# The last softmax chain of a fused attention and mixture kernel: reading from PSUM, turning over a diagonal, and small matmuls in the pauses

## The chip, the cores and the metric

The kernel runs on one core of one Trainium2 chip. The metric is device time in microseconds of one execution. A core has TensorE (matmul, with its own loading of weights), VectorE, ScalarE, GpSimd and SyncE; SyncE issues the DMA transfers here. PE, DVE, ACT, POOL and SP are the profile's names for them.

## The reference, cut to what matters

```python
def attn(q, k, v):                      # 4 batches, 8 heads, 576 tokens, 64 wide
    s = q @ k.T / 8
    s = where(s >= kth_largest(s, 32), s, -1e9)
    return softmax(s) @ v

def moe(x, phi, w1, w2):                # x 2304 x 512, 8 experts of 4 slots
    logits = x @ phi                    # 2304 x 32
    d = softmax(logits, axis=0)         # over all tokens, for each slot
    slot_input = d.T @ x                # 32 x 512
    slot_out[e] = relu(slot_input[e] @ w1[e]) @ w2[e]
    return softmax(logits, axis=1) @ slot_out

def moe2(x, w_in, w_out):
    h = x @ w_in
    g = where(h >= 1, h, where(h <= -1, 0, (h + 1) ** 2 / 4))
    return g @ w_out                    # 2304 x 512

out = moe2(moe(attn(q, k, v)))
```

## The kernel before

The attention runs over 16 pairs of heads (two heads at a time, four pairs for a batch), each in five rows of blocks of queries. Tokens of work (a letter for the step, two digits for row and half, the pair after the dot) are laid out in a repeating order for the frames, and for the last frames in a list written by hand, `TAIL`. In these stretches the order on TensorE, VectorE, ScalarE and GpSimd is exactly that of the list. The kernel's weights (w1, w2, w_out and helpers, 512 KB a tile, some loaded as two halves of 256 KB) come by a stream of loads from SyncE (`wload`, L196), in one fixed order, into buffers that come free during the attention. At most eight are in flight. Each load waits until what its buffer held is no longer read, and since SyncE issues in order, the loads behind wait with it.

The softmax over tokens is done batch by batch with a running maximum (`nmn`, negated), a running sum (`run_q`, then `run_s`) and a running weighted sum `acc` (partitions are pair and slot, columns the two heads' values): at each batch, acc = acc x al + new, where al is the exponential of the change of the maximum. For the last batch this chain stands at the end of `TAIL`, after the last attention matmuls (L550); it is called the drain here. It works in three pieces of tokens, n = 0 and 1 of 256 tokens each and n = 2 of the last 64 (the mid piece). The steps, with the lines of the kernel before, are:

- `na`, `nb`: logits of the piece on TensorE, one matmul for each of the four pairs of the batch, the last one in `nb` (L757). They go into one PSUM tile `lm_ps` of three banks, one bank for a piece.
- `nc`: ScalarE copies the logits to `lT` in SBUF (L760). `nl`: a copy of a part to `lall` for the later combine (L770).
- `nd`: VectorE takes the maximum (L764) and joins it to the running one (L765).
- `ne`: ScalarE's exponential into `eT`, with the sum (L773). `nf`: the factor `al` (L777).
- `nt`: TensorE turns `eT` (L782, and L285/L287 for the mid piece). `ng`: ScalarE copies the turned piece to `et` (L794) or `er` (L791).
- `nw`: the weighing, TensorE multiplies the turned exponentials with the tokens' values `xh` (L721), into the same bank. `nx`: VectorE, acc = acc x al + that (L798). `ny`: the running sum (L800).
- `jp`, `jd`: `run_q` of the earlier batches to `run_s`. `sp`: TensorE transposes `acc` to `si_ps` (L737). `sa`: ScalarE copies that to `siT` (L739).

With `siT` the experts begin: `h` from w1 (L1049), `so` from w2 (L1072), then the combine. The preparation of w_out (on ScalarE, GpSimd and VectorE) and moe2 follow, the last matmuls into `o_ps` (L1255).

Of the kernel before, what the change touches and what calls it, by code (L numbers as in the profile page):

```python
# [77 lines left out]
Y01.14 m09.11 C30.14 z4.14 O11.14 K10.14 T30.13 Q30.13 S31.14 U31.13 B0.14 L2.14 X10.14 K11.14  # L78
E31.13 m10.11 X11.14 C31.14 P00.14 G30.14 Y10.14 U40.13 T31.13 G31.14 M20.14 P01.14 Q31.13 M21.14
Y11.14 A20.13 L3.14 S40.14 R3.13 A21.13 O20.14 U00.14 K20.14 E40.13 C40.14 B1.14 O21.14 T40.13  # L80
Q40.13 X20.14 c0.15 c1.15 S00.15 E00.14 M30.14 K21.14 P10.14 T41.13 G40.14 H2.13 R4.13 U01.14 X21.14
V30.14 c4.15 Y20.14 K30.14 Q41.13 A30.13 P11.14 C00.15 T00.14 E01.14 S01.15 U10.14 Q00.14 M31.14
A31.13 C01.15 E10.14 U11.14 H3.13 Y21.14 T01.14 B2.14 Q01.14 R0.14 V31.14 Y30.14 S10.15 L4.14 X00.15
C10.15 T10.14 S11.15 P20.14 K31.14 Y31.14 E11.14 c5.15 U20.14 Q10.14 C11.15 A40.13 G01.15 P21.14
A41.13 H4.13 M40.14 L0.15 c2.15 B3.14 T11.14 V40.14 lD.13 S20.15 A00.14 U21.14 R1.14 A10.14 P30.14
K40.14 G10.15 E20.14 C20.15 M00.15 Q11.14 Y40.14 P31.14 lN.13 A01.14 T20.14 E21.14 Q20.14 S21.15
H0.14 M01.15 B4.14 A11.14 T21.14 U30.14 C21.15 O01.15 H1.14 S30.15 K01.15 R2.14 Q21.14 G11.15 K00.15
L1.15 E30.14 G20.15 lX.13 X01.15 T30.14 M10.15 U31.14 C30.15 A20.14 c6.15 E31.14 Y00.15 Y01.15
M11.15 B0.15 P40.14 Q30.14 S31.15 lC.13 C31.15 O11.15 U40.14 G21.15 X10.15 K10.15 L2.15 K11.15
T31.14 P01.15 R3.14 P00.15 M20.15 U01.15 A21.14 E40.14 Q31.14 U00.15 M21.15 V20.15 X11.15 S40.15  # L90
H2.14 T40.14 A30.14 E01.15 E00.15 Y10.15 Q40.14 Y11.15 G30.15 B1.15 C40.15 V21.15 A31.14 P10.15
H3.14 T41.14 T00.15 T01.15 U10.15 P11.15 R4.14 Q41.14 A40.14 K20.15 Q00.15 K21.15 A41.14 R0.15
G31.15 Q01.15 E10.15 L3.15 nm3.15 Y20.15 H4.14 P30.15 U11.15 A00.15 Y21.15 B2.15 lD.14 E11.15 A01.15
P20.15 M30.15 T10.15 T11.15 rd0.15 H0.15 R1.15 lY.13 Q10.15 G40.15 lE.13 P31.15 lN.14 M31.15 lX.14
V30.15 Q11.15 K30.15 lC.14 Y30.15 U20.15 E20.15 U30.15 fl0.15 A10.15 V31.15 A11.15 L4.15 rd1.15
lY.14 T30.15 K31.15 P21.15 lE.14 Y31.15 T20.15 H1.15 U31.15 M40.15 na0.15 Q30.15 Q20.15 fl1.15
U21.15 E21.15 T31.15 T21.15 R3.15 A30.15 Q31.15 nm4.15 V40.15 R2.15 K40.15 P40.15 Q21.15 Y40.15
U40.15 A31.15 B4.15 A20.15 A21.15 rd3.15 rd2.15 T40.15 B3.15 H3.15 xc1.15 xc0.15 H2.15 T41.15 Q40.15
Q41.15 R4.15 nb0.15 nc0.15 nd0.15 nl0.15 fl3.15 fl2.15 A40.15 xc2.15 A41.15 rd4.15 na1.15 ne0.15
# [10 lines left out]
def kernel_body(tc, qT, kT, vP, phi, w1, w2, w_in, w_out, out, fast, flag):  # L110
# [633 lines left out]
    def last_mix(k, n):  # L744
# [8 lines left out]
        turned = bank[:, :(NR + 1) * NSLOT].rearrange("p (r s) -> p r s", s=NSLOT)  # L753
# [7 lines left out]
        elif k == "d":  # L761
            mb = p_moe.tile([P, 1], F32, name="mb", tag="mb", bufs=3)
            nm = p_moe.tile([P, 1], F32, name="nmn", tag="nmn", bufs=4)
            nc.vector.reduce_max(mb, lT[:, c0:c1], axis=AX.X)  # L764
# [6 lines left out]
        elif k == "e":  # L771
            sb = p_moe.tile([P, 1], F32, name="sb", tag="sb", bufs=3)
            nc.scalar.activation(eT[:, c0:c1], lT[:, c0:c1], AF.Exp, bias=sums[n]["nm"], scale=1.0, accum_out=sb)  # L773
# [5 lines left out]
        elif k == "t":  # L779
            eye = ident[:NSLOT, :NSLOT]  # L780
            for r in main:
                nc.tensor.transpose(turned[:, r, :], eT[:NSLOT, r * P:(r + 1) * P], eye)  # L782
            if mid:
                for jj in range(2):
                    sl = slice(jj * REM, (jj + 1) * REM)
                    flip(turned[sl, NR, :], eT[:NSLOT, NR * P:], eye, jj)
        elif k == "g":
            if mid:
                for jj in range(2):
                    sl = slice(jj * REM, (jj + 1) * REM)  # L790
# [658 lines left out]
```

## Time and profile before

| | us |
|---|---|
| median of three runs | 773.25 (772.62 to 773.60) |
| the profiled execution | 771.83 |
| its span in the profile | 770.0 |
| TensorE busy | 736.8 (96%) |
| VectorE busy | 651.0 (85%) |
| ScalarE busy | 612.2 (80%) |
| GpSimd busy | 491.7 (64%) |
| chain that ended last: TensorE, VectorE, GpSimd, DMA | 58%, 24%, 7%, 6% |

A number of a view is from the profiled execution, in us from the start of its span. The busy share of an engine is a mean over stages that have different limits, so a change at one place is read in the rows of that place: which engine works, what the others wait for, and who waits for them. The stages that matter here: attention with the hand-written list to about 479 us, the drain to about 490, the experts to about 530, and moe2 to the end.

### The profile page before, as it was taken

The page shows a single profiled execution, that of the slowest core. Times are in us where ns is not written, and L with a number is a line of the kernel's source. Part 1 is how long each engine was busy: PE and PEld are TensorE (multiplying, and loading weights), DVE is VectorE, ACT ScalarE, POOL GpSimd, SP SyncE. Part 2 cuts the span into 40 slices and gives each one's busy share as a digit, 9 for nine tenths or more (in the row PEclk, how much of TensorE's full clock was granted, in tenths as well). Part 3 has the DMA queues.
Part 4 walks back from the last instruction along what each step waited for, and adds up shares of the span by engine and source line. Part 5 has one row for each costly group of instructions (what it writes and reads, how often), then busy time and mean ns, then how long its engine had stood idle before and what let it go on. Part 6 is the DMA issues. An engine that isn't in the chain of part 4 may idle for free.

```text
span 770.0 us, 15917 instructions
## 1 busy us (share of the span) xinstructions
PE 736.8 (96%) x5014; PEld 542.5 (70%) x5014; DVE 651.0 (85%) x2924; ACT 612.2 (80%) x1300; POOL 491.7 (64%) x532
## 2 busy tenths in 40 slices
PE   4899999999999999999999999898999999999996
PEld 2477777677777677777777788334577788888885
DVE  5999999999999999999999996173899967776662
ACT  4799999999999999999999997243788864554542
POOL 2899999999999999999999995030455400000000
PEclk9899999999999999999999999899999999999998
DMA  7414314304304302202202137999600020100101
GB/s 230 144 59 149 105 47 150 132 25 150 129 22 151 136 19 96 83 15 96 82 20 96 46 105 273 334 406 406 269 0 1 0 83 1 43 10 33 41 1 45
DMA packets 32013, 81.50 MB, mean 106 GB/s; under 512 B 5680, under 2 KB 6576, under 8 KB 31920
## 3 DMA queue, kind: packets, MB, share of 16 engines
q1 hardware_dynamic: 31632, 79.94, 29.1%
q8 instruction: 41, 0.67, 0.4%
...
q14 instruction: 52, 0.43, 0.2%
...
## 4 chain that ended last, share of the span: by engine, by line
PE 58%; DVE 24%; POOL 7%; DMA 6%; issue 2%; ACT 1%; SPq 1%; DVEq 0%; POOLq 0%; ACTq 0%
PE o_ps L1255 19%; PE av_ps L550 10%; PE s_ps L333 6%; PE pt_ps L509 6%; DVE cand L357 5%; DVE top L463 4%; DMA w<-in_moe_w_dram 3%; PE x_ps L333 3%; DVE ghl L1239 3%; POOL ssb L489 3%; DVE cand L362 2%; DVE top L364 2%; POOL mb L416 2%; PE av_ps L548 2%; PE h_ps L1207 2%
## 5 line engine op out<-in xcount | busy, mean ns | idle before, releaser
L1255 PE MATMUL o_ps<-whl,ghl 128*128 128x512 f32 x864 | 216.9, 395 | 1.3 <-DVE ghl L1221 0.5
L1255 PEld LDWEIGHTS o_ps<-whl,ghl 128*128 128x128 f32 x864 | 160.2, 188 | 38.1 <-DVE whl L1201 2.6
L489 POOL TENSOR_TENSOR ssb<-ssb,pen 128x576 f32<-128x576 f32 x141 | 180.3, 1283 | 2.9 <-ACT pen L486 0.4
L357 DVE MAX8 cand<-ssb 128x8 f32<-128x82 f32 (+1 forms) x1008 | 163.7, 235 | 5.4 <-ACT ssb L348 5.4
L550 PE MATMUL av_ps<-v_sb,ptb 128*128 128x65 f32 (+1 forms) x1280 | 143.0, 262 | 0.0
L550 PEld LDWEIGHTS av_ps<-v_sb,ptb 128*128 128x128 f32 (+1 forms) x1280 | 137.1, 181 | 6.3 <-issue 6.2
L1210 ACT ACTIVATE rg<-h_ps,half 128x384 f32<-128x384 f32 (+1 forms) x98 | 56.0, 572 | 68.3 <-PE h_ps L1207 68.3
L333 PE MATMUL s_ps<-kt,qt 64*128 64x288 f32 x512 | 99.5, 466 | 8.7 <-ACT ssb L348 4.4
L416 POOL TENSOR_SCALAR mb<-ssb,top 128x576 bf16<-128x576 f32 x62 | 106.9, 1724 | 0.9 <-DVE top L364 0.9
L348 ACT COPY ssb<-s_ps 128x576 f32<-128x576 f32 x144 | 95.4, 663 | 10.7 <-PE s_ps L333 9.5
L509 PE MATMUL pt_ps<-ident,ssb 128*128 128x128 f32 x600 | 93.8, 279 | 1.9 <-ACT ptb L525 1.8
L509 PEld LDWEIGHTS pt_ps<-ident,ssb 128*128 128x128 f32 x600 | 67.0, 146 | 29.5 <-ACT rs L533 6.8
L1227 DVE SCALAR_TENSOR_TENSOR rg<-h_ps,rg 128x384 f32<-128x384 f32 x95 | 52.7, 555 | 36.4 <-ACT rg L1211 36.3
L492 ACT ACTIVATE ssb<-ssb,kn 128x576 f32<-128x576 f32 x94 | 76.6, 816 | 0.1
L525 ACT COPY ptb<-pt_ps 128x512 f32<-128x512 f32 x120 | 73.0, 608 | 2.3 <-PE pt_ps L509 2.1
L486 ACT ACTIVATE pen<-ssb,kn 128x576 bf16<-128x576 f32 x94 | 73.8, 809 | 1.2 <-POOL kn L482 0.5
L463 DVE MAX8 top<-x_ps 128x8 f32<-128x584 f32 x94 | 71.1, 758 | 3.2 <-PE x_ps L447 2.8
L1190 POOL TENSOR_SCALAR tr_l<-tr_l 128x512 f32<-128x512 f32 x16 | 24.1, 1503 | 77.3 <-DVE tr_l L1189 77.3
L364 DVE MAX8 top<-cand 128x8 f32<-128x56 f32 x432 | 73.0, 206 | 0.1
L1239 DVE TENSOR_TENSOR ghl<-rg,ghl 128x384 fp32r<-128x384 f32 x95 | 67.7, 713 | 5.7
L453 POOL TENSOR_TENSOR w<-ssb,mb 128x576 f32<-128x576 f32 x50 | 64.6, 1293 | 1.2 <-DVE mb L413 1.2
L333 PEld LDWEIGHTS s_ps<-kt,qt 64*128 64x128 f32 x512 | 39.9, 190 | 34.6 <-ACT ssb L348 10.7
...
## 6 DMA issues: line engine op xcount, KB each, us to landing
w<-in_moe_w_dram SPq DMA_DIRECT2D x50, 512.0 KB, 6.7
x<-in_moe_w_in_dram SPq DMA_DIRECT2D x16, 512.0 KB, 3.8
w<-in_moe_w_out_dram SPq DMA_DIRECT2D x16, 512.0 KB, 10.3
w<-in_moe_w_dram SPq DMA_DIRECT2D x28, 256.0 KB, 5.7
...
out_dram<-o_sb SPq DMA_DIRECT2D x17, 256.0 KB, 2.3
```

Source lines behind the costliest of these rows:

```text
L333: nc.tensor.matmul(o, q[us], k[us, c:c + o.shape[-1]], start=True, stop=True, tile_position=(j * D, 0), skip_group_check=True)
L348: nc.scalar.copy(ssb[:, 0] if u[1] == NR else ssb[:, :, hf], st.pop((u, hf))[:, :, :HS])
L357: nc.vector.max(st[u]["cand"][:, j, 8 * g:8 * g + 8], row(u, j)[:, S * g // NSEG:S * (g + 1) // NSEG])
L364: nc.vector.max(t8, cand)
L416: nc.gpsimd.tensor_scalar(kept(u, j), row(u, j), t_u, None, op0=ALU.is_ge)
L463: nc.vector.max(st[u]["top"][:, j, TOPU:], src)
L489: nc.gpsimd.tensor_tensor(row(u, j), row(u, j), st.pop((u, "pen", j)), op=ALU.subtract)
L492: nc.scalar.activation(row(u, j), row(u, j), AF.Exp, bias=st[u]["kn"][:, j, 0:1], scale=0.125)
L509: nc.tensor.transpose(pt[:, c, :], pr[:, c0:c0 + P], ident)
L550: nc.tensor.matmul(o, pj[:, c, sl], v_sb[:, 4 * jj + c, :], start=False, stop=(c == NR - 1), skip_group_check=True)
L1239: nc.vector.tensor_tensor(gl, g, gh.bitcast(F32), op=ALU.subtract)
L1255: nc.tensor.matmul(pos[t][n], a[:, sl], w, start=(f == 0 and k == 0), stop=(f == NF - 1 and k == 2))
```

## The change

Seven things are changed.

1. `nd` and `ne` read the logits from PSUM (`lg`) instead of from `lT`. The copy `nc` is still made, for `lall`.
2. The turned exponentials get columns of their own in the bank, behind the logits and the weighing's result (from column 384).
3. `ng` of the pieces 0 and 1 is a copy on VectorE instead of ScalarE.
4. The mid piece's turned exponentials go by one ScalarE copy into a new tile `e_mid`. Its weighing is written the other way round: eight small matmuls (64 rows, 32 columns) add straight onto `si_ps`. `nx2` is gone.
5. `sp` is a matmul of `acc` with a diagonal matrix `grown`, which holds the mid piece's factor `al`; `dg` on VectorE makes it from `ident`. The tile `grown` is taken from the pool and the tag of the attention's tile `rs`.
6. `k3`, `k2`, `k4`, `k6`: 15 bf16 matmuls of 128 columns in all, with a result that nobody reads, between steps of the drain.
7. `TAIL` is written in another order, from its first token on (from about 424 us). `na1` stands well ahead of the last attention matmuls, where it stood behind them.

```diff
 TAIL = '''
-ng2.15 ny1.15 nw1.15 nw2.15 ny2.15 nx1.15 nx2.15 sp.15 sa.15
+ny0.15 ng2.15 k4.15 sp.15 ny1.15 ny2.15 nw2.15 k6.15 nl1.15 nl2.15 sa.15
...
+    e_mid = p_moe.tile([P, NSLOT], F32, name="e_mid")
+
     def slots_in(k):
-        if k == "p":
+        if k == "g":
+            last_ps["g"] = p_work.tile([P, P], F32, name="grown", tag="rs", bufs=3)
+            nc.vector.tensor_scalar(last_ps["g"], ident, sums[len(pieces) - 1]["al"], None, op0=ALU.mult)
+        elif k == "p":
             last_ps["s"] = ps_m.tile([P, P], F32, name="si_ps", tag="m_ps")
-            nc.tensor.transpose(last_ps["s"], acc, ident)
+            nc.tensor.matmul(last_ps["s"], acc, last_ps["g"], start=True, stop=True, skip_group_check=True)
...
-        turned = bank[:, :(NR + 1) * NSLOT].rearrange("p (r s) -> p r s", s=NSLOT)
+        turned = bank[:, 3 * P:3 * P + 2 * NSLOT].rearrange("p (r s) -> p r s", s=NSLOT)
...
-            nc.vector.reduce_max(mb, lT[:, c0:c1], axis=AX.X)
+            nc.vector.reduce_max(mb, lg, axis=AX.X)
...
-            nc.scalar.activation(eT[:, c0:c1], lT[:, c0:c1], AF.Exp, bias=sums[n]["nm"], scale=1.0, accum_out=sb)
+            nc.scalar.activation(eT[:, c0:c1], lg, AF.Exp, bias=sums[n]["nm"], scale=1.0, accum_out=sb)
...
         elif k == "g":
             if mid:
-                for jj in range(2):
-                    sl = slice(jj * REM, (jj + 1) * REM)
-                    nc.scalar.copy(er[sl, jj, :], turned[sl, NR, :])
-            if main:
-                lo, hi = main[0], main[-1] + 1
-                nc.scalar.copy(et[:, lo:hi], turned[:, lo:hi])
+                nc.scalar.copy(e_mid, turned[:, 0, :])
+            else:
+                nc.vector.tensor_copy(et[:, main[0]:main[-1] + 1], turned)
         elif k == "w":
-            weigh(pu, xs, et, main, mid)
+            if mid:
+                si = last_ps["s"]
+                for hp in range(NHP):
+                    for jj in range(2):
+                        sl = slice(jj * REM, (jj + 1) * REM)
+                        nc.tensor.matmul(si[sl, hp * NSLOT:(hp + 1) * NSLOT], xs[hp][0][sl, 8, :], e_mid[sl],
+                                         start=False, stop=True, skip_group_check=True)
+            else:
+                weigh(pu, xs, et, main, False)
...
+        elif name[0] == "k":
+            for _ in range(int(name[1:])):
+                nc.tensor.matmul(last_ps["t"][:, 0, 0], nbig, ident.bitcast(BF16)[:, :P], start=True, stop=True,
+                                 skip_group_check=True)
```

On TensorE the place is the end of the drain. Before, from the logits of the piece n = 1 on (`lx_ps` is a turn of the last tokens' values, `rq_ps` the step `jp`):

```order
L757 MATMUL lm_ps<-xT,phi_sb 128x256 x4
L287 MATMUL lx_ps<-ident,xh 64x64
L285 MATMUL lx_ps<-ident,xh 64x64
L782 MATMUL lm_ps<-ident,eT 128x32 x2
L757 MATMUL lm_ps<-xT,phi_sb 128x64 x4
L728 MATMUL rq_ps<-run_q,same 128x1
L721 MATMUL lm_ps<-xh,et 32x128 x8
L782 MATMUL lm_ps<-ident,eT 128x32 x2
L287 MATMUL lm_ps<-ident,eT 64x32
L285 MATMUL lm_ps<-ident,eT 64x32
L721 MATMUL lm_ps<-xh,et 32x128 x8
L721 MATMUL lm_ps<-xh,er 32x64 x8
```

Behind these stands only the transpose of `acc`, L737. Now, from the last attention matmuls to the logits of the mid piece:

```order
L550 MATMUL av_ps<-v_sb,ptb 64x65 x4
L762 MATMUL lm_ps<-xT,phi_sb 128x256
L787 MATMUL lm_ps<-ident,eT 128x32 x2
L728 MATMUL rq_ps<-run_q,same 128x1
L287 MATMUL lx_ps<-ident,xh 64x64
L285 MATMUL lx_ps<-ident,xh 64x64
L762 MATMUL lm_ps<-xT,phi_sb 128x64 x3
```

One logits matmul of 256 columns stands behind the attention instead of four, and the first turn follows it directly. The end of the drain now, from the last of the dummies `k4` to the first of `k6` (L912):

```order
L912 MATMUL lt_ps<-ident,nbig 128x128
L742 MATMUL si_ps<-grown,acc 128x128
L802 MATMUL si_ps<-e_mid,xh 64x32 x8
L912 LDWEIGHTS nbig
L912 MATMUL lt_ps<-ident,nbig 128x128
```

The mid piece's weighing stands behind the turn of `acc`, where it stood ahead of it, and its result has no way over VectorE any more.

On SyncE, the loads of weights around the first tiles of w_out (w_38 and w_39), with the semaphores that each waits for; DMAHW is the landing of an earlier transfer. Before:

```order
L196 DMA w_37_7714<-in_moe_w2_dram 128x512 [waits DMAHW0_49,Activation_49]
L196 DMA w_37_7715<-in_moe_w2_dram 128x512 [waits DMAHW1_49,Activation_49]
L196 DMA w_38_7857<-in_moe2_w_out_dram 128x1024 [waits DMAHW2_49,Activation_49]
L196 DMA w_39_7859<-in_moe2_w_out_dram 128x1024 [waits DMAHW3_49,Activation_49,Pool_49]
L196 DMA w_40_7861<-in_moe_w2_dram 128x1024 [waits DMAHW4_49,PE_49]
L196 DMA w_41_7863<-in_moe_w2_dram 128x1024 [waits DMAHW5_49]
L196 DMA w_42_7865<-in_moe_w2_dram 128x1024 [waits DMAHW6_49,PE_49]
```

And now:

```order
L196 DMA w_37_7719<-in_moe_w2_dram 128x512 [waits DMAHW0_49]
L196 DMA w_37_7720<-in_moe_w2_dram 128x512 [waits DMAHW1_49,Activation_49]
L196 DMA w_38_7873<-in_moe2_w_out_dram 128x1024 [waits DMAHW2_49,PE_49]
L196 DMA w_39_7875<-in_moe2_w_out_dram 128x1024 [waits DMAHW3_49,Activation_49,Pool_49]
L196 DMA w_40_7877<-in_moe_w2_dram 128x1024 [waits DMAHW4_49,Activation_49]
L196 DMA w_41_7879<-in_moe_w2_dram 128x1024 [waits DMAHW5_49]
L196 DMA w_42_7881<-in_moe_w2_dram 128x1024 [waits DMAHW6_49,PE_49]
```

The order of the loads is the same; the load of w_38 waits for TensorE where it waited for ScalarE. Its buffer lies over the place of the tag `rs`.

## Rows read from the trace of the kernel before

**Rows 1.** Windows: stretch, us, busy us by engine (instructions), TensorE clock, DMA share, GB/s

```profile
424.00:481.00 57.00, 56.42 (x454) 46.20 (x452) 49.38 (x239) 50.80 (x117) 47.07 (x54) 1.00 0.43 141
```

**Rows 2.** Timeline of TensorE in the drain: start, us, instruction, count, idle before it, releaser

```profile
478.73 0.34 PE L550 MATMUL av_ps<-v_sb,ptb 128*64 128x65 f32 x3
478.99 1.99 PE L757 MATMUL lm_ps<-xT,phi_sb 128*128 128x256 f32 x8
...
481.35 0.31 PE L782 MATMUL lm_ps<-ident,eT 32*128 32x32 f32 x2
481.58 0.88 PE L757 MATMUL lm_ps<-xT,phi_sb 128*128 128x64 f32 x6
483.04 0.43 PE L757 MATMUL lm_ps<-xT,phi_sb 128*128 128x64 f32 x2 [0.58 <-ACT xT L628]
...
483.89 0.64 PE L721 MATMUL lm_ps<-xh,et 128*32 128x128 f32 x16 [0.25 <-ACT lT L760]
...
488.93 0.45 PE L737 MATMUL si_ps<-ident,acc 128*128 128x128 f32 x1 [1.01 <-DVE acc L798]
489.73 1.08 PE L1049 MATMUL h<-w,siT 128*32 128x512 f32 x4 [0.35 <-ACT siT L739]
```

**Rows 3.** Timeline of ScalarE in the drain

```profile
482.50 0.37 ACT L760 COPY lT<-lm_ps 128x256 f32<-128x256 f32 x1 [2.62 <-PE lm_ps L757]
...
483.73 0.52 ACT L773 ACTIVATE eT<-lT,nmn 128x256 f32<-128x256 f32 x1
...
484.38 0.35 ACT L773 ACTIVATE eT<-lT,nmn 128x64 f32<-128x64 f32 x1
...
485.36 0.21 ACT L794 COPY et<-lm_ps 128x64 f32<-128x64 f32 x1 [0.35 <-PE lm_ps L285]
```

**Rows 4.** Timeline of VectorE in the drain

```profile
482.91 0.42 DVE L764 TENSOR_REDUCE mb<-lT 128x1 f32<-128x256 f32 x1 [3.43 <-ACT lT L760]
483.36 0.16 DVE L765 SCALAR_TENSOR_TENSOR nmn<-mb,nmn 128x1 f32<-128x1 f32 x1
483.87 0.22 DVE L764 TENSOR_REDUCE mb<-lT 128x1 f32<-128x64 f32 x1 [0.35 <-ACT lT L760]
...
488.05 0.73 DVE L798 SCALAR_TENSOR_TENSOR acc<-acc,al,lm_ps 128x128 f32<-128x128 f32 x2 [1.33 <-PE lm_ps L721]
```

**Rows 5.** Windows as in rows 1, of the drain's end, the experts and moe2

```profile
486.00:490.00 4.00, 2.22 (x37) 1.59 (x41) 1.32 (x6) 0.61 (x3) 0.00 (x0) 0.50 1.00 328
490.00:493.00 3.00, 3.00 (x20) 0.62 (x16) 0.00 (x0) 0.00 (x0) 0.00 (x0) 0.54 0.94 369
500.00:520.00 20.00, 19.80 (x164) 7.56 (x157) 14.04 (x23) 9.46 (x19) 5.84 (x4) 1.00 1.03 405
560.00:570.00 10.00, 9.79 (x43) 7.39 (x41) 10.00 (x17) 8.39 (x18) 5.72 (x5) 1.00 0.00 0
```

**Rows 6.** Groups by form, one VectorE operation from PSUM, from SBUF: busy us, mean ns

```profile
L463 DVE MAX8 top<-x_ps 128x8 f32<-128x584 f32 x94 | 71.1, 758 | 3.2 <-PE x_ps L447 2.8
L463 DVE MAX8 top<-w 128x8 f32<-128x584 f32 x50 | 37.7, 756 | 6.7 <-POOL w L472 6.7
```

**Rows 7.** Timeline of SyncE: the issues of w_38 and w_39

```profile
480.46 0.86 SPq L196 DMA_DIRECT2D w<-in_moe_w_out_dram  x2
```

**Rows 8.** DMA issues at 458.5, 471.2, 480.0, 493.6, 518.0 in turn: us to landing last

```profile
w<-in_moe_w_dram SPq DMA_DIRECT2D x1, 512.0 KB, 4.0
w<-in_moe_w_dram SPq DMA_DIRECT2D x1, 512.0 KB, 3.6
w<-in_moe_w_dram SPq DMA_DIRECT2D x1, 256.0 KB, 5.8
w<-in_moe_w_dram SPq DMA_DIRECT2D x1, 512.0 KB, 7.0
w<-in_moe_w_dram SPq DMA_DIRECT2D x1, 256.0 KB, 6.6
```

**Rows 9.** Timeline of TensorE at the experts' second product

```profile
525.79 1.04 PE L1072 MATMUL so<-w,h1T 128*32 128x512 f32 x8
```

More of the change, by code (lines that the diff above doesn't have):

```diff
@@ L77 @@
 TAIL = '''
[L78 to L99, printed above, removed]
@@ L100 @@
-xc3.15 H4.15 nb1.15 fl4.15 nt0.15 na2.15 nc1.15 xc4.15 nd1.15 nb2.15 nf0.15 jp.15 ng0.15 nc2.15
-nd2.15 nw0.15 ne1.15 ne2.15 jd.15 ny0.15 nt1.15 nl2.15 nt2.15 nf2.15 nl1.15 ng1.15 nx0.15 nf1.15
-ng2.15 ny1.15 nw1.15 nw2.15 ny2.15 nx1.15 nx2.15 sp.15 sa.15
+m09.11 z4.14 U31.13 C30.14 T30.13 Y01.14 O11.14 S31.14 K10.14 Q30.13 B0.14 L2.14 X10.14 K11.14
+C31.14 U40.13 E31.13 X11.14 m10.11 P01.14 M20.14 S40.14 c0.15 E40.13 Y10.14 T31.13 P00.14 G30.14
+A20.13 M21.14 Q31.13 O20.14 G31.14 T40.13 R3.13 A21.13 Q40.13 U00.14 Y11.14 C40.14 T41.13 O21.14
@@ new lines @@
+L3.14 B1.14 c1.15 K20.14 S00.15 K21.14 U01.14 H2.13 X20.14 M30.14 C00.15 R4.13 E00.14 S01.15 c4.15
+V30.14 M31.14 X21.14 Q41.13 P10.14 G40.14 A40.13 V31.14 P11.14 A41.13 C01.15 Y20.14 T00.14 E01.14
+U10.14 A30.13 Y21.14 Q00.14 L4.14 H4.13 K30.14 A31.13 E10.14 B2.14 U11.14 P20.14 T01.14 H3.13 S10.15
+Y30.14 Q01.14 K31.14 c5.15 X00.15 C10.15 G01.15 P21.14 S11.15 U20.14 Y31.14 R0.14 T10.14 E11.14
+L0.15 A00.14 Q10.14 B3.14 U21.14 E20.14 T11.14 lD.13 C11.15 A01.14 M00.15 lN.13 Q11.14 c2.15 M40.14
+S20.15 R1.14 M01.15 H0.14 T20.14 E21.14 G10.15 A10.14 C20.15 K00.15 Q20.14 G11.15 V40.14 A11.14
@@ new lines @@
+O01.15 P30.14 L1.15 S21.15 K01.15 K40.14 T21.14 H1.14 C21.15 U30.14 lX.13 P31.14 Y40.14 X01.15 R2.14
+M10.15 Q21.14 U31.14 S30.15 E30.14 Y00.15 A20.14 lC.13 B4.14 K10.15 M11.15 P40.14 G20.15 lY.13
+C30.15 A21.14 Y01.15 E31.14 c6.15 T30.14 G21.15 O11.15 S31.15 H2.14 Q30.14 B0.15 X10.15 L2.15 K11.15
+C31.15 U40.14 T31.14 lE.13 P00.15 X11.15 M20.15 R3.14 P01.15 U00.15 S40.15 Y10.15 E40.14 U01.15
+Y11.15 Q31.14 A30.14 C40.15 G30.15 E00.15 T40.14 B1.15 V20.15 A31.14 M21.15 Q40.14 E01.15 T41.14
+G31.15 K20.15 H3.14 P11.15 V21.15 T00.15 Y20.15 R4.14 P10.15 T01.15 K21.15 L3.15 Q41.14 A40.14
@@ new lines @@
+U10.15 R0.15 Q00.15 A41.14 Q01.15 A00.15 H4.14 U11.15 M30.15 E10.15 A01.15 lD.14 lN.14 E11.15 T10.15
+rd0.15 G40.15 T11.15 H0.15 V30.15 Q10.15 lX.14 M31.15 R1.15 Q11.15 fl0.15 nm3.15 A10.15 lC.14 K30.15
+Y21.15 P30.15 Y30.15 B2.15 lY.14 xc0.15 V31.15 A11.15 lE.14 U30.15 P20.15 na1.15 P31.15 L4.15 K31.15
+U20.15 P21.15 rd1.15 Y31.15 H1.15 T30.15 U21.15 M40.15 na0.15 Q30.15 E20.15 U31.15 V40.15 E21.15
+fl1.15 T20.15 xc1.15 T31.15 K40.15 Q20.15 nm4.15 Y40.15 nb0.15 R3.15 Q31.15 T21.15 nd0.15 B4.15
@@ L103 @@
+B3.15 A30.15 R2.15 Q21.15 ne0.15 A31.15 P40.15 A20.15 rd3.15 U40.15 H3.15 A21.15 T40.15 rd2.15
+T41.15 H2.15 Q40.15 fl3.15 R4.15 fl2.15 Q41.15 A40.15 xc2.15 xc3.15 A41.15 nb1.15 rd4.15 nt0.15
+H4.15 nd1.15 jp.15 fl4.15 ng0.15 ne1.15 jd.15 na2.15 xc4.15 nf1.15 nc0.15 k3.15 nb2.15 nt1.15 nf0.15
+nd2.15 nw0.15 ng1.15 ne2.15 nl0.15 nw1.15 nf2.15 nx0.15 nc1.15 dg.15 nc2.15 k2.15 nt2.15 nx1.15
+ny0.15 ng2.15 k4.15 sp.15 ny1.15 ny2.15 nw2.15 k6.15 nl1.15 nl2.15 sa.15
 '''.split()
@@ L780, in last_mix @@
             eye = ident[:NSLOT, :NSLOT]
[L781 to L782 removed]
+            for n_, r in enumerate(main):
+                nc.tensor.transpose(turned[:, n_, :], eT[:NSLOT, r * P:(r + 1) * P], eye)
             if mid:
                 for jj in range(2):
[L785 to L786 removed]
+                    flip(turned[jj * REM:(jj + 1) * REM, 0, :], eT[:NSLOT, NR * P:], eye, jj)
         elif k == "g":
             if mid:
[L789 to L796 removed]
+                nc.scalar.copy(e_mid, turned[:, 0, :])
+            else:
+                nc.vector.tensor_copy(et[:, main[0]:main[-1] + 1], turned)
+        elif k == "w":
+            if mid:
[7 more added lines that the diff above has]
+                weigh(pu, xs, et, main, False)
         elif k == "x":
```

2 lines of the change are left out of this document (1 added, 1 removed).

## The prediction

> **What bounds the kernel now.** I read the profile from the place of the change outwards. First the windows by engine over the stretch in which the order of work differs: TensorE is busy for 56.42 of the 57.0 us from 424 to 481 at full clock [rows 1]. Up to there its own work is the bound; a new order can regain at most 0.58 us of idle, while any matmul moved ahead of the last attention matmul costs its whole time. That last one ends at 479.07 (call it X) [rows 2].
>
> Then the drain, by the timelines of three engines. After X no step has enough of its own work; it is one chain of hand-offs: logits, maximum, exponential, turn, copy, weighing, sum, transpose, copy [rows 2 to 4]. From X to the first expert matmul at 489.73 it takes 10.66 us. The reader should see how short each step is (0.2 to 0.9 us), and that the next starts 0.03 to 0.15 us after the one it waits for: the first copy to lT ends at 482.87 and the maximum starts at 482.91; the last sum ends at 488.78 and `sp` starts at 488.93. [...]
>
> Last the weight transfers, since the expert matmuls live on them. From 500 to 520 the DMA engines are always busy at 405 GB/s [rows 5], which is 1.29 us for a 512 KB tile. At 526 TensorE uses tiles almost as they land: the 256 KB half of w_65 issued at 518.03 lands 6.6 us later, at 524.6 [rows 8], and the fourth of the eight matmuls that begin at 525.79 [rows 9], at some 526.2, is its first reader. I take the slack as 1.62 us, the least of any tile in the trace. The stream has no gap by which it could catch up before 526, and I found none behind it: VectorE is busy without pause on the w_out preparation afterwards (10.00 of 10 us from 560 on [rows 5]), and TensorE is the bound to the end. So the end of the kernel follows the later of two things: TensorE's arrival with the expert work, and the stream of weights with 1.62 us in hand.
>
> **The change part by part.**
>
> *Order ahead of X.* Three 256-column matmuls of `na1` move from behind X to ahead of it. The eight records of 1.99 us are four such matmuls [rows 2], so 0.48 us each and 1.45 us for three. Against that stands the regained idle, 0 to 0.58. X becomes 479.07 + 1.45 - (0 to 0.5) = 480.0 to 480.5; I take 480.25, 1.2 later than now.
>
> *The chain from X to sp.* The copies to lT leave the chain in front of the maximum and the exponential, but `lm_ps` is one tile of three banks, and on each engine its readers and writers still wait for one another in the order of the list. I add along that order. (a) `nb1` 0.48, `nt0` 0.31, `nd1` 0.42 + 0.16, `ng0` about 0.2 (as ScalarE's `ng` of 0.21 [rows 3]; on VectorE it has no row: 0.15 to 0.35), `ne1` 0.52: 2.09, with hand-offs 2.29. (b) `na2` 0.88, `nc0` 0.37 (now behind `na2`), `nb2` 0.22 (half of the pair of 0.43), `nt1` 0.31: 1.78, with hand-offs 1.98. (c) `nd2` 0.22 + 0.16, `nw0` 0.64, `ng1` 0.2, `ne2` 0.35, `nw1` 0.64: 2.21, with hand-offs 2.71. (d) `nx0` 0.37 (half of the 0.73 of two), `nc1` 0.37, `nc2` 0.2, `nt2` 0.31 as `nt0`, `nx1` 0.37, `sp` 0.45 or a little less at full clock: 2.07, with hand-offs 2.48. Sum from X to the end of `sp`: 9.46; before, 10.31 (489.38 - 479.07). (e) The mid piece's eight small matmuls about 0.6 (as `nw0`), and from their end to the first expert matmul 0.35, which is what TensorE idles there now [rows 2]: 1.0. Sum 10.46 against 10.66. The gain of the chain is therefore only 0.2 us, because the mid weighing now stands behind `sp`, while 1.2 us were moved ahead of X: expert matmuls begin at 480.25 + 10.46 = 490.7, 1.0 later than now.
>
> A maximum read from PSUM could be dearer than one from SBUF. Two rows of one form say not: 584 elements from PSUM take 758 ns, from SBUF 756 ns [rows 6]; I add nothing. [...]
>
> *The matmuls on the diagonal and the dummies.* `grown` is one VectorE operation beside the copies (hidden while `nt2` is late; 0.2 if not). The 15 dummies are bf16 of 128 columns; this trace has no row of them. The nearest are the 128-column float32 `sp` at 0.45 and the 64-column logits at 0.22, so 0.05 to 0.3 each; they stand in pauses, and the last four of a group can delay `sp` or the copy by 0 to 0.4, in the range. What they can give is the clock: at full clock the stretch 490 to 493 needs 1.5 us less for the same work [rows 5], and the weighing 0.4 less.
>
> *The weight queue.* This is where I expect the loss. The tile `grown` takes a buffer of the ring that held `rs`, and the first w_out tile, w_38, is loaded over that place. Before, this load waited for a ScalarE copy and was issued at 480.46 [rows 7]; the order shows that it now waits for TensorE, and counting the semaphore to its wait value gives the matmul `sp` that reads `grown`. SP issues in order, so w_39, w_40 and w_41 stand behind it. The transfer ahead of it, issued at 479.99, lands 5.8 us later, at 485.8 [rows 8]: from there the DMA engines have nothing until `sp` ends, at T = 480.25 + 9.46 = 489.7. A load issued into an empty queue lands 3.6 and 4.0 us after its issue [rows 8]; I take 3.7. The ninth tile from there, w_46, lands at T + 3.7 + 8 x 1.28 = T + 13.94 = 503.6. Before, issued at 493.6, it landed after 7.0 us, at 500.6 [rows 8]. The stream is 3.0 us late, 1.62 of them are slack, so 1.35 us are lost if nothing else is late; with the low clock in the chain, `sp` falls 0.3 to 0.6 later, and the loss is up to 1.95. I take 1.6. The price runs from T = 486.7, where the stream is on time, up one for one.
>
> **The rivals.**
>
> A, the forecast: the stream restarts at `sp`, +0.6 to +2.6 us (X and the hand-offs, 0.5 each way, restart 3.6 to 4.0). Chance 0.50.
>
> B: the clock falls later, in the expert matmuls, as it does now. Then TensorE's arrival is 1.0 late, plus 0.5 to 1.2 for a longer low stretch and dummies in front of the copy, while the tiles at 526 are 1.35 to 1.95 behind their slack; the two partly add as +2.2 to +2.9. For: the clock is low there now. Against: the dummies are meant for these pauses. Chance 0.15. [...]
>
> C: the tail is not later. If the new order fills all of TensorE's idle and X stays near 479.1 to 479.6, T is 488.6 or, with 0.5 to 1 us shorter hand-offs, 487.6; the stream is 0.9 to 1.9 late, slack takes 1.62 of it, and nothing or 0.3 is lost; TensorE gains by the clock until it meets the stream, 0.7 at most. -0.8 to +0.5. For: the first items of the list after the divergence could close gaps. Against: only 0.58 us of gaps exist [rows 1]. Chance 0.18.
>
> D, the other side: the chain is shorter than my serial sum. Were `na2` (0.88), `nc0` (0.37) and two hand-offs beside the chain and not on it, and X at 479.1, `sp` would end at 479.1 + 9.46 - 1.45 - 0.4 = 486.7. From this T on the stream is not late at all, the expert matmuls start 2 us earlier at full clock, and the 1.62 us of slack at 526 become the gain: -1.6 to -2.3. For: each reads a bank of its own. Against: the tile is shared, and three matmuls moved ahead of X. Chance 0.12.
>
> E: the list as a whole stalls TensorE somewhere in 424 to 481, where 57 us of it are reordered: +3 to +5. Against: both ScalarE and VectorE have room there. Chance 0.05.
>
> **How the numbers follow.** A is the likeliest: 773.25 + 1.6 = 774.9 us, taken to the median. The profiled execution took 771.83 us around a span of 770.0, 1.42 less than the median, so in its own terms 773.4. A range that leaves out at most 2 in 10 goes from the lower end of C, 773.25 - 0.8 = 772.4, to 776.9, which holds B and the bounds of A; out of it are D and most of E, 0.17. A measurement of this kernel can tell about 0.2% from no change, 1.55 us, borders at 771.7 and 774.8. A lies across the upper one, 0.27 above and 0.23 below. Slower: 0.27 + 0.15 + 0.05 = 0.47. Same: 0.23 + 0.18 = 0.41. Faster: 0.12.
>
> **What would show it.** Right: between about 486 and 490 the DMA share falls to nearly nothing, w_38 is issued when the matmul with `grown` ends, w_46 lands near 503.6, and around 527 TensorE waits for the expert weights. The last attention matmul ends at 480.0 to 480.5, `sp` at 489.2 to 490.2. Wrong would be: w_38 issued before 482; a stream without a gap; `sp` done by 487; TensorE not waiting at 527 though the stream is 3 us late, which would mean that slack lies behind that I did not see; or a clock below full from 490 to 493 with the wait at 527 gone.

## The result and the profile after

The changed kernel takes 778.38 us (median of six runs, 777.03 to 779.61) against 773.02 us of the kernel before in the same session; the ratio is 1.0068, with a 95% interval from 1.0057 to 1.0078. It is slower by 5.3 us. Forecast was slower by 1.6, with a range to 776.9: the sign is right, and the size forecast is a third of what was measured. Its profiled execution took 778.39 us around a span of 776.6.

TensorE up to the end of the attention (in the kernel before this was [rows 1]), and two stretches of the drain; the columns are those of [rows 1]:

```profile
424.00:482.50 58.50, 56.41 (x453) 46.31 (x455) 50.71 (x239) 51.33 (x116) 47.14 (x55) 1.00 0.40 127
486.00:490.00 4.00, 2.69 (x30) 1.74 (x32) 0.90 (x4) 1.05 (x5) 0.00 (x0) 0.50 0.37 138
490.00:493.00 3.00, 2.25 (x26) 1.22 (x18) 1.02 (x5) 0.62 (x3) 0.00 (x0) 0.50 0.00 0
493.00:499.00 6.00, 5.85 (x41) 2.83 (x45) 1.15 (x6) 0.32 (x2) 0.00 (x0) 0.50 0.70 253
```

TensorE now idles 2.1 us before the last attention matmul ends, where it idled some 0.6. From 490 to 493 no weights move at all (DMA share 0.00). The clock is at 0.50 from 486 to 499, longer than in [rows 5], where it was back to 0.54 on the mean of 490 to 493 and full soon after.

The chain on TensorE, after the change (start, us, instruction, count, idle before it and who ended that), to be laid beside [rows 2]:

```profile
481.84 0.69 PE L550 MATMUL av_ps<-v_sb,ptb 128*64 128x65 f32 x10
...
484.89 0.97 PE L762 MATMUL lm_ps<-xT,phi_sb 128*128 128x64 f32 x6 [0.76 <-ACT eT L778]
...
487.75 1.08 PE L721 MATMUL lm_ps<-xh,et 128*32 128x128 f32 x16 [0.39 <-DVE mb L769]
489.62 1.08 PE L721 MATMUL lm_ps<-xh,et 128*32 128x128 f32 x16 [0.78 <-ACT eT L778]
...
491.77 0.26 PE L287 MATMUL lm_ps<-ident,eT 32*64 32x32 f32 x1 [0.75 <-ACT lT L765]
...
492.89 0.80 PE L742 MATMUL si_ps<-grown,acc 128*128 128x128 f32 x2
493.62 1.07 PE L802 MATMUL si_ps<-e_mid,xh 64*64 64x32 f32 x16
494.62 0.82 PE L912 MATMUL lt_ps<-ident,nbig 128*128 128x128 bf16 x6
495.59 1.08 PE L1062 MATMUL h<-w,siT 128*32 128x512 f32 x4
```

Read the brackets. The logits of the mid piece (L762, 64 columns) need nothing from the exponential of another piece, and yet they wait 0.76 us for it; the first weighing waits for the maximum of another piece; the second for another exponential; the turn of the mid piece for a copy to `lT`. The first three pairs have in common only the PSUM tile `lm_ps`, in which each piece has a bank of its own. The copy that the turn waits for is of the mid piece's own logits, in other columns of the same bank. The experts begin at 495.59 instead of 489.73, 5.9 us later.

The stream of weights, as issues on SyncE, and the time to landing of the transfers issued at 493.72 (w_38) and 499.69 (w_46), beside [rows 7, 8]:

```profile
482.93 0.90 SPq L196 DMA_DIRECT2D w<-in_moe_w_dram  x2
493.72 0.80 SPq L196 DMA_DIRECT2D w<-in_moe_w_out_dram  x2
```

```profile
w<-in_moe_w_out_dram SPq DMA_DIRECT2D x1, 512.0 KB, 3.6
w<-in_moe_w_dram SPq DMA_DIRECT2D x1, 512.0 KB, 9.0
```

w_38 is issued when the matmul with `grown` has ended (493.69), as forecast; w_46 lands at 508.7 instead of 500.6, 8.1 us late instead of 3.0. At the place of [rows 9] TensorE meets it. The twenty records (a matmul is two) that took 2.33 us from 525.36 on before take 3.04 us now, and the last tile of w2 is used 0.04 us after its landing:

```profile
531.51 3.04 PE L1085 MATMUL so<-w,h1T 128*32 128x512 f32 x20
```

So two things are late, and by nearly as much: TensorE, which uses each weight tile 6.15 us later than before up to this place, and the stream, 8.0 us late with 1.62 in hand. From the two, the end is 6.6 us late in this pair of spans. Some 0.75 us of this is not the change's: ahead of the first altered token TensorE is that late in this execution already (the attention matmuls of L550 that begin at 415.99 before begin at 416.73). And the profiled execution of the kernel before was 1.2 us faster than its median, so the 5.3 us of the medians is the figure to explain. The experiments take the two apart.

### The profile page after: what moved, and what is told of

It is laid out like the page before. It is cut to its first block, busy times and chain, and to the rows that moved or that the text cites. A ratio compares the mean times of both kernels' runs of the same rounds, so it can differ in the third digit from the quotient of the medians.

```text
span 776.6 us, 15942 instructions
## 1 busy us (share of the span) xinstructions
PE 744.4 (96%) x5015; PEld 547.2 (70%) x5030; DVE 652.4 (84%) x2926; ACT 611.7 (79%) x1297; POOL 491.0 (63%) x532
## 4 chain that ended last, share of the span: by engine, by line
PE 58%; DVE 25%; POOL 7%; DMA 5%; ACT 3%; issue 2%; ACTq 0%; POOLq 0%; DVEq 0%; SPq 0%
PE o_ps L1268 19%; PE av_ps L550 10%; PE s_ps L333 7%; PE pt_ps L509 6%; DVE cand L357 5%; DVE top L463 5%; DMA w<-in_moe_w_dram 3%; PE x_ps L333 3%; POOL ssb L489 3%; DVE ghl L1252 3%; DVE cand L362 2%; POOL mb L416 2%; DVE top L364 2%; PE h_ps L1220 2%; DVE mb L413 2%
## 5 line engine op out<-in xcount | busy, mean ns | idle before, releaser
L550 PE MATMUL av_ps<-v_sb,ptb 128*128 128x65 f32 (+1 forms) x1280 | 143.1, 261 | 0.0
L550 PEld LDWEIGHTS av_ps<-v_sb,ptb 128*128 128x128 f32 (+1 forms) x1280 | 137.1, 181 | 5.5 <-issue 5.4
L333 PE MATMUL s_ps<-kt,qt 64*128 64x288 f32 x512 | 101.2, 473 | 9.2 <-ACT ssb L348 4.9
```

The source lines that it names most:

```text
L333: nc.tensor.matmul(o, q[us], k[us, c:c + o.shape[-1]], start=True, stop=True, tile_position=(j * D, 0), skip_group_check=True)
L550: nc.tensor.matmul(o, pj[:, c, sl], v_sb[:, 4 * jj + c, :], start=False, stop=(c == NR - 1), skip_group_check=True)
```

## The experiments

Ratios are to the kernel before, with 95% intervals; where us are given for a ratio, it is its distance from 1 times 772.6.

### One thing taken back from the changed kernel

**own_buf**: the diagonal in a tile that no load waits for.

```diff
-            last_ps["g"] = p_work.tile([P, P], F32, name="grown", tag="rs", bufs=3)
+            last_ps["g"] = same.rearrange("p r s -> p (r s)")
```

> The changed kernel with the diagonal matrix written into the tile `same`, which is free by then, so that the load of w_38 no longer waits for the transpose. If the late weight stream makes the loss (my prediction), w_38 is issued by about 484 and most of the 5.4 us come back: 773 to 774 us. If TensorE's own late arrival makes it (the expert matmuls start 5.9 us later and every weight tile up to 526 is used 6.15 us later, long after it has landed), only what the stream adds behind that comes back, 0.3 to 0.7 us: 777.7 to 778.1 us, and the expert matmuls still start near 495.6.

Measured 776.85 us, ratio 1.0043 (1.0029 to 1.0058): about 1.9 us came back, more than the 0.3 to 0.7 expected if TensorE's lateness makes the loss, and much less than the five expected if the stream does. In its profile the experts begin as late as in the changed kernel, and each tile is used 6.1 us late, with 2.28 us or more in hand (the profiled execution took 778.61, well above the median, so the 1.9 us can't be read in it):

```profile
494.99 0.82 PE L912 MATMUL lt_ps<-ident,nbig 128*128 128x128 bf16 x6
495.96 1.08 PE L1062 MATMUL h<-w,siT 128*32 128x512 f32 x4
```

The held load alone does not make the loss. TensorE's own lateness does as much or more.

**old_order**: all code of the change, its own drain, but the attention tokens and `na1` as before.

```diff
-... Q41.15 A40.15 xc2.15 xc3.15 A41.15 nb1.15 rd4.15 nt0.15 H4.15 nd1.15 ...
+... nb0.15 nd0.15 fl3.15 fl2.15 A40.15 xc2.15 A41.15 rd4.15 na1.15 ne0.15 xc3.15 H4.15 nb1.15 nt0.15 nd1.15 ...
```

> All code of the change, its drain from the first turn on in the changed order, but the attention tokens and `na1` in the order of the kernel before. In the changed kernel the last attention matmul ends 3.4 us later, of which 1.45 are the three matmuls of `na1` and some 2 are idle time of TensorE. If the order is to blame for the 2 us, the last attention matmul ends at 479.1, the chain is 1.45 longer, and the time falls by about 2 us to 776.4 us. If the order is innocent (the late arrival comes from the drain alone), the time stays at 778.

778.68 us, 1.0067 (1.0049 to 1.0086): nothing came back. The last attention matmul did end at 479.1, and the experts began earlier, at 495.21, with tiles used 4.95 us late instead of 6.15. But the clock fell earlier, before 484 (0.88 from 482 to 484, 0.50 after), and the stream, restarted at 493.3 by the same wait, caught TensorE at 532: slack 0.04 us, and behind that place TensorE is 7.2 us late.

**no_dummies**: the changed kernel without its 15 dummies.

```diff
-... nc0.15 k3.15 nb2.15 ... nc2.15 k2.15 nt2.15 ... ng2.15 k4.15 sp.15 ny1.15 ny2.15 nw2.15 k6.15 nl1.15 ...
+... nc0.15 nb2.15 ... nc2.15 nt2.15 ... ng2.15 sp.15 ny1.15 ny2.15 nw2.15 nl1.15 ...
```

> The changed kernel without its 15 dummy matmuls. They stood while the granted clock was at half anyway (from 486 to 499). If they do nothing, the only thing that changes is that the last six of them no longer stand between the copy to siT (ends 495.0) and the first expert matmul (495.6): -0.5 us, 777.9 us. If they shorten the low stretch, it gets longer without them and the time rises by up to 1.5 us.

778.50 us, 1.0070 (1.0052 to 1.0088): no change that the interval can show. Here too TensorE came earlier (experts at 494.13, tiles used 4.46 us late), and the stream took it back:

```profile
532.01 2.56 PE L1085 MATMUL so<-w,h1T 128*32 128x512 f32 x12 [0.74 <-DMA w<-in_moe_w_dram]
```

**own_none**: no dummies, and the diagonal in `same`, the two edits above together.

> The changed kernel with both taken out: the diagonal matrix in the tile `same`, so that w_38 does not wait for the transpose, and no dummies. Without the dummies TensorE came to the experts 4.46 us late instead of 6.15, but the late stream took that gain back at 526 (slack 0.04). If the two late arrivals stand beside each other, each hiding the other, now the gain appears: every tile is used some 4.5 us later than before, no slack near 0, about 777.2 us. If the stream had nothing to do with it, 778.5 as without dummies alone.

777.15 us, 1.0062 (1.0045 to 1.0079). In its profile what was expected is there: tiles are used 4.2 us late throughout, no slack is under 2, and the span is 774.3. Its median is 777.15, and the intervals of own_none, own_buf and no_dummies overlap. The traces show the two late arrivals each hiding the other; how many tenths each takes off in the median is not settled.

**own_none_old**: own_none with the attention tokens as before.

> As own_none, with the attention tokens in the order of the kernel before. There the first chain step after the attention began 1.0 us earlier (second logits matmul at 481.45 instead of 482.43). With no stream in the way this is now gained: some 3.5 us over the kernel before, 776.3 us. If the order of the attention is without effect, as own_none.

777.03 us, 1.0051 (1.0034 to 1.0068). With the old order, no held load and no dummies, what is left of the change is the code of the drain with its order from the first turn on, and it alone still costs 3.9 us. That is the largest part, and my prediction had it as a gain of 0.2. The old order of the attention gained nothing here over own_none (I expected 776.3), as it gained nothing in old_order.

### One thing of the change put into the kernel before

**new_order_old_code**: the kernel before with the attention tokens and `na1` in the changed order.

```diff
-... A40.15 xc2.15 A41.15 rd4.15 na1.15 ne0.15 xc3.15 H4.15 nb1.15 fl4.15 nt0.15 na2.15 ...
+... A40.15 xc2.15 xc3.15 A41.15 nb1.15 rd4.15 H4.15 nl0.15 fl4.15 nt0.15 na2.15 ...
```

> The kernel before (copies to lT, maximum and exponential from SBUF, weighing of the mid piece as before, no dummies, no diagonal), with the attention tokens and `na1` in the changed order, and its own drain from the turn on. If the order costs 2 us, 775.0 us, and the last attention matmul ends near 482.5; w_38 then waits only for a ScalarE copy, so the stream is late by the same 3.4 us less its slack. If the order costs nothing, 773 us or less.

774.67 us, 1.0020 (1.0010 to 1.0029): on the kernel before, the order costs 1.5 us. The waits of TensorE from 424 to 482 (what waited for what: us, times, longest) are those that the changed kernel has too, 1.8 us together; before, there was one such wait of 0.5:

```profile
PE lt_ps L509 <- ACT ptb L525: 0.8, 1, 0.8
PE s_ps L333 <- ACT ssb L348: 0.5, 1, 0.5
PE lt_ps L509 <- ACT ssb L492: 0.5, 1, 0.5
```

**hold_w38**: the kernel before, with w_38 held until the transpose ends.

```diff
+            last_ps["g"] = p_work.tile([P, P], F32, name="grown", tag="rs", bufs=3)
+            nc.vector.tensor_copy(last_ps["g"], ident)
...
-            nc.tensor.transpose(last_ps["s"], acc, ident)
+            nc.tensor.transpose(last_ps["s"], acc, last_ps["g"])
```

> The kernel before with a copy of the unit matrix in a buffer of the ring of `rs`, used only by the transpose of `acc`: w_38 is held until the transpose ends at 489.4, all else is as before. This is the stream's price by itself, as the prediction summed it: restart at 489.4, w_46 lands at 489.4 + 13.9 = 503.3 instead of 500.6, 2.7 late less 1.62 of slack, +1.1 us: 773.7 to 774.2 us. If the restart is dearer (in the changed kernel it took 15.0 us from the transpose to the landing of w_46), +2.2 us.

775.54 us, 1.0037 (1.0023 to 1.0051): 2.9 us by the held load alone. TensorE is not late at all on its way to 526 (experts at 489.58), so this is the mechanism of the prediction by itself. The DMA queue runs dry, and TensorE then waits for a weight:

```profile
486.00:490.00 4.00, 2.38 (x37) 1.59 (x41) 1.19 (x5) 0.45 (x3) 0.00 (x0) 0.50 0.00 0
```

```profile
527.84 2.56 PE L1074 MATMUL so<-w,h1T 128*32 128x512 f32 x12 [0.92 <-DMA w<-in_moe_w_dram]
```

The restart is dearer than I summed. Us to landing (last column) of the transfers issued at 489.29 (w_38), at 490.19 (w_40), and of those at 490.19 and 490.62 (w_40, w_41) together, by their median:

```profile
w<-in_moe_w_out_dram SPq DMA_DIRECT2D x1, 512.0 KB, 3.6
w<-in_moe_w_dram SPq DMA_DIRECT2D x1, 512.0 KB, 5.2
w<-in_moe_w_dram SPq DMA_DIRECT2D x2, 512.0 KB, 6.3
```

The first lands at 492.9 and the third at 495.4, so 1.28 apart from tile to tile. For the two of the last row to have 6.3 in the middle, the second of them took 7.4: the fourth tile lands at 498.0, 2.6 behind the third. w_46 lands 15.2 us after the transpose, not 13.9. The queue did not stand still for that. Between those two landings the DMA engines were busy throughout and moved nearly two tiles:

```profile
495.42:497.99 2.57, 2.57 (x28) 0.72 (x24) 0.00 (x0) 0.00 (x0) 0.00 (x0) 1.00 1.00 400
```

In the trace a load reports its landing in sixteen parts, and the matmul at 527.84 starts 0.04 us after the last part of its tile. Of the first three tiles the sixteen come within 0.6 us. Of the fourth, fifteen have come by 496.68 and one comes at 497.99, and of each tile up to w_46 one part stays 1.3 us behind. In just this stretch falls a packet of another queue, that of the instructions (16 KB, from 495.16, 0.94 us long). DMA queues from 495 to 496 (packets, MB, share):

```profile
q1 hardware_dynamic: 98, 0.38, 94.0%
q8 instruction: 1, 0.02, 5.9%
```

The changed kernel has the same, with the packet at 499.23 and one part of the fourth tile and of the later ones 1.15 us behind. It is no matter of the restart: in the kernel before, whose stream was not held, the packet at 481.14 is followed by a tile with fifteen parts landed by 482.45 and the last at 483.82. That the packet delays one part in sixteen fits all of these; no run leaves the packet out, so it is not shown as the cause.

**psum_reads**: the kernel before, with maximum and exponential reading PSUM. Here the late copies to `lT` find columns that the turn has overwritten, so the logits for the combine are not those of the reference; the work is the same.

```diff
-            nc.vector.reduce_max(mb, lT[:, c0:c1], axis=AX.X)
+            nc.vector.reduce_max(mb, lg, axis=AX.X)
...
-            nc.scalar.activation(eT[:, c0:c1], lT[:, c0:c1], AF.Exp, bias=sums[n]["nm"], scale=1.0, accum_out=sb)
+            nc.scalar.activation(eT[:, c0:c1], lg, AF.Exp, bias=sums[n]["nm"], scale=1.0, accum_out=sb)
...
-... na2.15 nc1.15 xc4.15 ... ng0.15 nc2.15 nd2.15 ... nt1.15 nl2.15 ... nl1.15 ... nw2.15 ny2.15 ...
+... na2.15 xc4.15 ... ng0.15 nd2.15 ... nt1.15 ... nw2.15 nc1.15 nc2.15 nl1.15 nl2.15 ny2.15 ...
```

> The kernel before with one part of the change: maximum and exponential read the logits from PSUM, and the two later copies to lT stand behind the weighing. The three pieces still share one PSUM tile. If reading from PSUM couples the pieces (an exponential of one piece must wait for matmuls of another and the other way round), the drain gets longer by 1 to 3 us although two copies are off its path: 774 to 776 us. If the reads are free of that, it gets 0.4 to 0.8 us shorter: 772 us.

775.95 us, 1.0048 (1.0032 to 1.0064). It is slower by 3.7 us, but I had put `nl1` and `nl2` ahead of the last sums on VectorE, so a part of that could be my placing.

**psum_reads2**: the same with the turn in columns of its own, as in the change, and `nl1`, `nl2` behind `sp`.

> As psum_reads (one shared tile, maximum and exponential from PSUM), with two things mended that muddied it: the turned exponentials have columns of their own, and the copies to lall stand behind the transpose, where they stood in front of the last sums on VectorE and held them up by some 1 us. If the coupling through the shared tile is the cost, the false waits of psum_reads remain (0.8 us of logits for a copy of other columns and an exponential, 0.7 and 0.4 for maxima, 1.0 for an exponential) and it is slower than before by 1.5 to 2.5 us: 774 to 775 us. If psum_reads was slow only by the misplaced copies, 772 us.

776.27 us, 1.0050 (1.0033 to 1.0067), no better. The misplaced copies were not it; the forecast of 774 to 775 was still too low. Its waits from 479 to 493 on TensorE:

```profile
PE si_ps L737 <- DVE acc L798: 1.5, 1, 1.5
PE lm_ps L721 <- ACT er L791: 1.1, 1, 1.1
PE lm_ps L782 <- ACT eT L773: 1.0, 1, 1.0
PE lm_ps L757 <- ACT xT L631: 0.8, 1, 0.8
PE lm_ps L757 <- DVE mb L764: 0.7, 1, 0.7
PE lm_ps L721 <- DVE mb L764: 0.4, 1, 0.4
```

Four of them (1.1, 1.0, 0.7, 0.4) are waits of a matmul into `lm_ps` that end with a step of another piece on ScalarE or VectorE; the kernel before had the first of them too. In the kernel before, the readers of that tile were the copies to `lT`, 0.2 to 0.4 us each [rows 3]; now they are the maximum with its hand-off and the exponential of 0.5 us, and every matmul for another piece stands behind them.

### The shared tile taken apart

**split_before**: the kernel before, with one PSUM tile for each piece.

```diff
-        if "b" not in last_ps:
-            last_ps["b"] = ps_s.tile([P, 3, 512], F32, name="lm_ps", tag="x_ps", bufs=1)
-        bank = last_ps["b"][:, n]
+        if ("b", n) not in last_ps:
+            if n == 0:
+                last_ps["b", n] = ps_s.tile([P, 3, 512], F32, name="lm0_ps", tag="x_ps", bufs=1)[:, 0]
+            elif n == 1:
+                last_ps["b", n] = ps_s.tile([P, 2, 512], F32, name="lm1_ps", tag="s_ps", bufs=1)[:, 0]
+            else:
+                last_ps["b", n] = ps_m.tile([P, 512], F32, name="lm2_ps", tag="m_ps")
+        bank = last_ps["b", n]
```

> The kernel before with nothing changed but a PSUM tile of its own for each piece. There the second weighing waits for a ScalarE copy of the mid piece (1.08 us) that itself waits for VectorE's sum of another piece. If the shared tile holds this drain too, 0.5 to 1.2 us less than before: 772 us. If it reads from SBUF and so is not held, 773.

769.47 us, 0.9961 (0.9944 to 0.9977): 3.0 us faster than the kernel before, with no instruction of the computation changed. More than forecast, since the experts begin at 486.75 instead of 489.73. Each piece had a bank of its own already, so it is the tile that tied them together. The second weighing, before and in this run, shows the wait that is gone; it takes 0.64 instead of 1.08 us, since the clock is still full from 484 to 486 here and was at 0.50 from 486 on before:

```profile
486.41 1.08 PE L721 MATMUL lm_ps<-xh,et 128*32 128x128 f32 x16 [1.08 <-ACT er L791]
484.47 0.64 PE L721 MATMUL lm_ps<-xh,et 128*32 128x128 f32 x16
```

**split_old**: own_none_old with the same edit.

> As own_none_old, with a PSUM tile of its own for each of the three pieces instead of one tile of three banks. In the changed kernel the logits of the mid piece wait for the exponential of another piece (0.8 us), the weighing for a maximum (0.4), the second weighing for an exponential (0.8), the mid piece's turn for a copy to lT (0.75 to 1.07): each only since they share a tile. If these false waits make the drain long, the first expert matmul begins near 488 instead of 495, and the time is 771.5 to 774 us, at or below the kernel before. If the drain is long by its own steps, it stays near own_none_old.

768.35 us, 0.9948 (0.9931 to 0.9965): some 8 us less than own_none_old with its 1.0051, and 4 us less than the kernel before. The waits of TensorE from 479 to 488 and the window of the whole drain. Of the four bracketed waits of the changed kernel the three between pieces are gone; the one left (L287) is between the mid piece's own copy and turn:

```profile
PE lm_ps L287 <- ACT lT L770: 0.6, 1, 0.6
PE h L1067 <- ACT siT L744: 0.4, 1, 0.4
```

```profile
482.00:492.00 10.00, 9.03 (x112) 4.90 (x115) 3.46 (x18) 2.84 (x13) 0.00 (x0) 1.00 1.00 393
```

TensorE is busy for 9.03 of 10 us and the clock is full; in the kernel before it was 6.62 at 0.70 in the same window. The experts begin at 487.37. Now the stream is the bound: at 522.8 a tile is used 0.04 us after it has landed.

**split_held**: split_old with `grown` in the ring of `rs` again.

```diff
-            last_ps["g"] = same.rearrange("p r s -> p (r s)")
+            last_ps["g"] = p_work.tile([P, P], F32, name="grown", tag="rs", bufs=3)
```

> As split_old (768.4 us), but the diagonal matrix is again in the place that w_38 is loaded over, so that the stream restarts only when the transpose has read it, near 486.4. By the sum of the prediction w_46 then lands 13.9 us later, near 500.4 where split_old has 498.9, and since split_old already used a tile 0.05 us after its landing, the whole 1.4 us are lost: 769.8 us. If the stream does not bind, 768.4.

771.81 us, 0.9988 (0.9978 to 0.9997): the held load costs 3.1 us here, more than the 1.4 forecast. w_46 landed at 502.4, 15.4 us after the transpose, where the sum of the prediction said 13.9.

**split_psum** and **split_psum2**: psum_reads and psum_reads2 with the tile split. The first has the same altered columns as psum_reads.

> As psum_reads, but each piece has a PSUM tile of its own. If the coupling through the shared tile is all that the reads from PSUM cost, they now give what they promise over split_before (769.5 us): the copies of 0.4 and 0.2 us leave the path, 768.0 to 769.0 us. If a read from PSUM is itself dear, 770 us or more.

> As psum_reads2 with a PSUM tile for each piece, to be compared with split_before (769.5 us). If reading from PSUM is a gain once the pieces are apart, TensorE's arrival comes 0.5 to 1 us earlier than in split_before and the stream, held by nothing, follows: 768 to 769 us. If a read from PSUM gives nothing by itself, 769.5; if it costs, 770 or more.

split_psum: 770.57 us, 0.9968 (0.9956 to 0.9980), above the forecast, since the misplaced `nl1` held the last sum (TensorE waited 1.56 us for it). split_psum2: 768.77 us, 0.9941 (0.9925 to 0.9958), as forecast. With the pieces apart the reads from PSUM cost nothing (768.77 us against 769.47 of split_before); that they gain over split_before is not settled, as the intervals overlap. With the tile shared the same code gave 1.0050. So the loss is not in the read but in the tile.

**split_dummies**: split_before, with nine dummies in short pauses around the transpose.

```diff
-... nw1.15 nw2.15 ny2.15 nx1.15 nx2.15 sp.15 sa.15
+... nw1.15 nw2.15 k6.15 ny2.15 nx1.15 nx2.15 sp.15 sa.15 k3.15
```

> split_before with nine bf16 dummies, six in the pause of 0.64 us before the transpose of `acc` and three after it. In split_before the granted clock fell to half for 487 to 491. If dummies in short pauses keep it full, the expert matmuls lose 1 to 1.5 us less and the time is near 768.3 us; if the clock does not care for them, 769.5.

768.66 us, 0.9945 (0.9928 to 0.9961), against 0.9961 (0.9944 to 0.9977). In its profile the clock is full from 482 to 492, where it was 0.83 in split_before:

```profile
482.00:492.00 10.00, 9.39 (x121) 5.10 (x125) 3.23 (x15) 2.97 (x15) 0.00 (x0) 1.00 1.03 405
```

But split_psum2 has a full clock there (1.00) without a dummy, so this doesn't show that the dummies did it, and the times overlap.

## Why the prediction was right or wrong

*The stream.* Right: w_38 behind the transpose, SyncE stopped behind it, the DMA queue empty, TensorE meeting the stream at the tiles of 526. hold_w38 shows it alone: 2.9 us. Two terms were mis-sized. The restart brought w_46 at T + 15.0 to 15.4, not T + 13.94: I spaced all tiles by 1.28, and one part in sixteen of the fourth tile and of those behind it came 1.05 to 1.3 us later, about a tile's time. And of the slack of 1.62 only some 1.2 counted: in hold_w38 the stream is 3.88 late and the work behind it 2.67.

*X.* Wrong by 2.27 us. I let the new order only regain idle, 0 to 0.58, and took 480.25. It ended at 482.52, 3.46 later than before: 0.75 was there ahead of the list in this execution, 1.45 is `na1`, and some 1.3 are new waits of TensorE in the list (1.8 less 0.5). So 1.5 of the 2.27 is the forecast's own miss. That was rival E (a new order that stalls), which I had at 0.05; new_order_old_code prices it at 1.5 us. A list of 350 tokens in which every engine is at 8 to 10 tenths is no place to expect only gains.

*The chain.* Here the step failed that mattered most: "9.46 from X to `sp`", and with it "the gain of the chain is therefore only 0.2". It took 11.2 us, and to the experts 13.1 instead of 10.46. I had the serial order by the shared tile in the sum, but three sizes were wrong. The durations were those at full clock, while the clock fell shortly before 486, in front of both main weighings (1.08 and 1.08 instead of 0.64 each), the transpose and the mid piece's weighing (1.07, where split_old has 0.66 at full clock). The matmul with `grown` is two records with 0.80 where the transpose was one with 0.45, also at half clock. And the six dummies of `k6` stand between the copy to siT (ends 495.0) and the experts (495.59), which costs some 0.2 against the hand-off of 0.35. I named the low clock in the chain as 0.3 to 0.6; by the rows at either clock (0.44 for each weighing, 0.41 for the mid piece's, 0.31 for the matmul with `grown`, the rest in logits and turns) it was some 2, an estimate. The sum took 0.64 for the second weighing, although the kernel before had 1.08 there. own_none_old shows that the drain's code costs 3.9 us with everything else put back, psum_reads2 that the reads from PSUM are enough for as much, and split_psum2 that they cost nothing once the pieces do not share a tile (768.77 us against 769.47 of split_before).

*The clock.* Rival B had the clock fall in the expert matmuls; it fell before them and stayed low for their first 3.4 us. The rows show a granted clock of 0.50 from 486 to 499 with the dummies in place, and no_dummies, at 0.50 from 488 to 496 without them, is no slower. In split_old and split_psum2 it is full from 482 to 492, with TensorE busy for 9.03 and 8.64 of the 10 us, against 6.62 at 0.70 before. That the dummies would keep the clock full was my estimate: the changed kernel, at 0.68 in the same window with TensorE busy for 7.18 us, disagrees with it, and no run shows what keeps the clock full. Why split_before, busy for 8.78 of the 10 us, has 0.83 there is not settled.

*PSUM against SBUF.* The maximum over 256 columns took 0.42 us from SBUF [rows 4] and takes 0.42 from PSUM:

```profile
483.43 0.42 DVE L769 TENSOR_REDUCE mb<-lm_ps 128x1 f32<-128x256 f32 x1 [0.51 <-PE lm_ps L787]
```

So adding nothing for the source of the maximum was right. What the source cost here was not its own latency but whom it held up: the reads from PSUM gave 1.0050 on one shared tile (psum_reads2) and 0.9941 with a tile for each piece (split_psum2).

*The sum.* By single parts on the kernel before, the order costs 1.5, the reads from PSUM 3.9 and the held load 2.9: 8.3 us, where the whole change costs 5.3. They don't add. In the traces of old_order and no_dummies the stream takes back at 532 what TensorE had gained, so the two latenesses stand beside each other; and the order, 1.5 us on the kernel before, gave nothing back when it was undone in the changed code. How the 5.3 us divide among the parts is therefore not settled. I had forecast the stream as the only loss. What rival D asked for (pieces that do not wait for each other, `sp` done by 486.7) is what the split gives: `sp` ends at 486.4 in split_old, and the time is 768.35, 4 us less than before.
